# Converting the fold's 64-bit tiles in pairs of 1024 columns, with the buffers around them laid out in pairs

## The chip, the cores and the metric

One core of one Trainium2 chip runs the whole kernel. The metric is device microseconds from start to end of one execution; the kernel before was timed three times. The trace is of one further execution. The engines are named as the profile names them: PE is the matrix engine, with PEld for its weight loads, DVE the vector engine, ACT the scalar engine, POOL the GpSimd engine, SP the engine whose queue issues nearly all DMA transfers.

## The reference

Attention with pooled keys and values feeds two dense layers. For 8 batches, 8 heads, 576 tokens and 64 columns per head:

```
k_p, v_p = mean over 8 neighbouring tokens of k, v        # 72 of each per head
attn = softmax(q @ k_p.T / 8); x = attn @ v_p             # laid out as 4608 tokens x 512
x = ((x @ w1) * (x @ w2) @ w3) @ w_out                    # 512 -> 1024 -> 1024 -> 512
out = square(relu(x @ w_in)) @ w_out2                     # 512 -> 2048 -> 512
```

The weights come as 64-bit floats (`setup_inputs` multiplies float32 draws by 64-bit scalars), q, k and v as 32-bit floats.

## The kernel before, in words

Every large product is made of numbers split into a high and a low part, three matmuls for each product of tiles. Since nothing stands between `w3` and `w_out`, the kernel first multiplies these two into one matrix W: this is the **fold** (`fold`, L697). Then come nine blocks of 512 tokens (`stage_ab`, L828, and `stage_w`, L862), then the second layer.

A 64-bit weight tile of 128 x 512 numbers is 512 KB. `load64` (L142) loads it as 32-bit word pairs. `words` (L149) runs two ACT instructions over it: L152 scales the high words in place, L153 writes the scaled low words into the float32 tile `w`. `join` (L155) runs three DVE instructions: L161 (shift), L162 (sign and bits together) and L164 (integer addition into `w`). Each of the five covers 512 columns.

The fold converts 32 tiles: 16 of w3, 8 of w_out and the 8 first halves (512 columns) of w1 and w2. It walks over 64 matmul positions (`mms`, L709). At each position the steps put there by `conv` (L739) are emitted, then one float32 matmul (L819, two PE instructions in the profile), then one `tick()`, which lets attention work in. A conversion is `act` (ACT), one position later the join (DVE); for w3 two more steps, `turn` (four PE transposes, L759) and `copy` (ACT, L765); for w1 and w2 `hi` (ACT cast, L770) and `lo` (DVE subtraction, L774). A tile that a matmul needs is begun at least five positions before its first use. Tiles of w1 and w2 begin at position 14 and every 6 positions after (`W12_AT`, `W12_GAP`), and `act` of conversion n issues loads up to conversion n + 3 (`PRE` = 4, L743). The queues keep one order for each engine, which the compiler's list scheduler makes from this order of emission and from when it believes each instruction to be ready.

Buffers: raw word pairs go to `x_p` (8 buffers of 4 KB per partition) until the first x tile of the attention exists, then to `sec_p` (4 of 4 KB). The float32 `w` of w3 lies in two small tiles of `tmp_p`, that of w1 and w2 in the three `cg` tiles of `tmp_p`, w_out in `prep_p`. Split w1 and w2 go to `w0_p` (8 of 4 KB). The three buffers of `raw_p` hold the k and v tiles of batches after the first (`kv_parts`, L302) and, from the end of the fold on, the raw second halves of w1 and w2 (`second_half`, L1303). Keys of batch 1 may be loaded from position 44 on (L807). Each k tile is summed over its tokens by DVE (L330), copied by POOL (L352) and transposed by PE (`pe_kt`, L381).

Attention of batch 0 runs as side work through the fold: scores, softmax (ACT L486), transposes, and products that write x (L547, L550). After the fold, around 113 us, the first block of `stage_ab` begins, with the second halves of w1 and w2 converted tile by tile beside it.

Of the kernel before, what the change touches and what calls it, by code (L numbers as in the profile page):

```python
# [8 lines left out]
F32 = mybir.dt.float32  # L9
F32R = mybir.dt.float32r  # L10
U32 = mybir.dt.uint32
# [9 lines left out]

LEAD = 3

PRE = 4

W12_AT = 14

W12_GAP = 6

LAG = 2  # L30

# [4 lines left out]
def attn_moe_moe2_kernel(  # L36
# [58 lines left out]
    at_p = tc.alloc_tile_pool(name="att", bufs=1, side="right")  # L95


# [43 lines left out]

    def load64(src, pool):  # L142

        tag = "x" if pool is x_p else "w" if pool is prep_p else "raw"
        r = pool.tile([P, TB, 2], U32, tag=tag, name="raw")
        nc.sync.dma_start(r, src.bitcast(U32).rearrange("p (c t) -> p c t", t=2))
        return r

    def words(r, w):  # L149

        hf = r.bitcast(F32)[:, :, 1]
        nc.scalar.activation(hf, hf, ACTF.Copy, scale=2.0 ** -112)  # L152
        nc.scalar.activation(w.bitcast(U32), r[:, :, 0], ACTF.Copy, scale=2.0 ** -29)  # L153

    def join(r, w):  # L155


        u = r.rearrange("p (y c) t -> p y (c t)", y=2)[:, :, :TB // 2]
        lo, hi = (r[:, :, i].rearrange("p (y c) -> p y c", y=2) for i in range(2))
        wu = w.bitcast(U32).rearrange("p (y c) -> p y c", y=2)  # L160
# [103 lines left out]

    def xt_tile(blk, c):
        if (blk, c) not in xt:
            xt[blk, c] = x_p.tile([P, 2, TB], F32R, tag="x", name=f"x_{blk}_{c}")
        return xt[blk, c]

    tasks = []  # L270
# [153 lines left out]
    def load_q(b, hf):  # L424


        if b < EARLY:
            for i in HALF[hf]:
                s1, n = QT[i]
                if b == 0:  # L430
                    if i % 2 == 0:
                        q_nat["w"] = w0_p.tile([P, 2, H, D], F32, tag="w", name="q_nat")
                    r = q_nat["w"][:, i % 2]
# [263 lines left out]
    def fold():  # L697
# [14 lines left out]
        for pos, (m, f) in enumerate(mms):  # L712
            use.setdefault(("w3", f, m // nh), pos)
            use.setdefault(("wo", m), pos)
        begin = {}
        nxt = len(mms)
        for key, pos in sorted(use.items(), key=lambda z: -z[1]):
            begin[key] = nxt = min(pos - 5, nxt - (2 if nxt > 1 else 1))
        w12 = [("w12", n, kc) for kc in range(KD) for n in range(2)]
        for j, key in enumerate(w12):  # L720
            begin[key] = W12_AT + W12_GAP * j
        convs = sorted(begin, key=lambda key: begin[key])
        raws = {}
        n_load = [0]

        def load(upto):
            while n_load[0] < min(upto, len(convs)):
                key = convs[n_load[0]]
                n_load[0] += 1
                if key[0] == "w3":  # L730
                    _, f, h = key
                    src = w3[f * P:(f + 1) * P, h * TB:(h + 1) * TB]
                elif key[0] == "wo":
                    src = wo[key[1] * P:(key[1] + 1) * P, :]
                else:
                    src = (w1, w2)[key[1]][key[2] * P:(key[2] + 1) * P, :TB]
                raws[key] = load64(src, early_pool())

        def conv(n, key):  # L739
            st = {}  # L740

            def act():
                load(n + PRE)  # L743
                if key[0] == "w3":
                    st["w"] = tmp_p.tile([P, TB], F32, tag=("gf", "a")[key[2] % 2], name="w32")
                elif key[0] == "wo":
                    y, x = divmod(key[1], 2)
                    if y not in wo_t:
                        wo_t[y] = prep_p.tile([P, 2, TB], F32, tag="w", name="wo")
                    st["w"] = wo_t[y][:, x, :]  # L750
# [4 lines left out]
            def turn():  # L755
                st["ps"] = ps = ps_mm.tile([P, TB], F32, tag="mm", name="ps_w3")
                for c in range(nh):
                    cs = slice(c * P, (c + 1) * P)
                    nc.tensor.transpose(ps[:, cs], st["w"][:, cs], ident)  # L759

            def copy():
                _, f, h = key
                if f not in w3t:
                    w3t[f] = g_p.tile([P, nm, P], F32, tag="g", name="w3t")
                nc.scalar.copy(  # L765
                    w3t[f][:, h * nh:(h + 1) * nh, :].rearrange("p m f -> p (m f)"), st["ps"])

            def hi():
                st["t"] = w0_p.tile([P, 2, TB], F32R, tag="w", name="wt")
                nc.scalar.copy(st["t"][:, 0, :], st["w"])  # L770

            def lo():
                t = st["t"]
                nc.vector.tensor_sub(t[:, 1, :], st["w"], f32(t[:, 0, :]))  # L774
                nm_ = ("w1", "w2")[key[1]]
                wt[nm_, key[2], 0] = t
                done.add((nm_, key[2], 0))

            steps = [act, lambda: join(raws.pop(key), st["w"])]
            steps += {"w3": [turn, copy], "wo": [], "w12": [hi, lo]}[key[0]]  # L780
            for x, fn in enumerate(steps):
                put(begin[key] + x, fn)

        for n, key in enumerate(convs):
            conv(n, key)

        def merged(f):
            t = wW_p.tile([P, 2, TB], F32R, tag="w", name="Wt")
# [489 lines left out]
    def po_step(i, u):  # L1278
# [21 lines left out]
            load_wide(u + len(WIDE))  # L1300
        drop((i, u))

    def second_half(x, nm_, w, kc):  # L1303

        st_ = {}
# [7 lines left out]

        def hi():

            pool, tag = (sec_p, "raw") if x < 4 else (prep_p, "w")
            wt[nm_, kc, 1] = t = pool.tile([P, 2, TB], F32R, tag=tag, name="wt2")
            nc.scalar.copy(t[:, 0, :], st_["w"])  # L1318

        def lo():  # L1320
# [66 lines left out]
    for i in range(NB):  # L1387
# [4 lines left out]
        for u in range(U1):  # L1392
# [4 lines left out]
            stage_ab(i, u)  # L1397
            if i == last and u == TB // P - 1:
                for n in ("B11", "T1", "T2", "T3"):
                    for x in range(2):  # L1400
                        x2o[n, x] = w0_p.tile([P, 2, TB], F32R, tag="w", name="x2o")
                raw_x.append(x_p.tile([P, 2, TB], F32, tag="x", name="x2r"))
# [121 lines left out]
```

## Time and profile before

| what | value |
|---|---|
| three timed runs | 1513.43, 1515.6, 1517.6 us (median 1515.6) |
| the profiled execution, its own time | 1516.18 us |
| its span, first to last instruction | 1514.4 us |
| PE busy | 1477.3 us (98%) |
| DVE, ACT, POOL busy | 998.1, 795.9, 81.2 us |
| mean granted PE clock | 0.998 |

The span is what the trace covers; 1.8 us of the profiled execution lie around it. Busy shares are means over the span: the fold is its first 113 us, and shares there differ from the mean. [...]

### The profile page before, as it was taken

The numbers are of one execution on the slowest core, as the hardware profiler recorded it, in microseconds if no ns is written. First come the engines' busy times: TensorE is split into PE (matmuls) and PEld (weight loads), VectorE is DVE, ScalarE is ACT, GpSimd is POOL, SyncE is SP. The second block draws the span as 40 slices with busy tenths as digits, with TensorE's granted clock in tenths as the row PEclk, the third lists the DMA queues.
The fourth block names the chain that finished last, engine by engine and source line by source line (L and its number), as shares of the span: only waits on it lengthen the run. The fifth ranks groups of instructions, "written<-read, shape, count | busy, mean of one in ns | idle before, by whom it ended". The sixth has DMA issues, their size and how long they took to land.

```text
span 1514.4 us, 21299 instructions
## 1 busy us (share of the span) xinstructions
PE 1477.3 (98%) x6752; PEld 1196.1 (79%) x6752; DVE 998.1 (66%) x1798; ACT 795.9 (53%) x1953; POOL 81.2 (5%) x145
## 2 busy tenths in 40 slices
PE   6899999999999999999999999999999999999998
PEld 3457788887888887888887878888888888888887
DVE  7988776777557367374266787659675967576542
ACT  6966464545435346363246764556445644554431
POOL 1011111111010011010000000000000000000000
PEclk9999999999999999999999999999999999999999
DMA  9554666757557457465349987778777877788752
GB/s 289 200 147 137 174 187 173 204 145 220 135 159 217 143 149 208 111 191 163 102 153 338 338 276 237 208 208 234 231 208 206 234 207 206 207 273 282 211 157 90
DMA packets 292783, 301.34 MB, mean 199 GB/s; under 512 B 119360, under 2 KB 184896, under 8 KB 292672
## 3 DMA queue, kind: packets, MB, share of 16 engines
q1 hardware_dynamic: 287488, 290.54, 65.8%
q10 hardware_dynamic: 5184, 9.44, 1.7%
q8 instruction: 55, 0.90, 0.3%
q14 instruction: 56, 0.46, 0.1%
HBM read 243.27 MB, written 56.62 MB: 198 GB/s over the span
## 4 chain that ended last, share of the span: by engine, by line
PE 76%; DVE 10%; ACT 6%; DMA 5%; issue 2%; SPq 1%; ACTq 0%; DVEq 0%
PE ps_w L194 20%; PE o L1231 18%; PE acc L194 9%; PE ps_a L1129 5%; PE ps_c L1129 5%; PE ps_d L1129 5%; PE ps_h L194 3%; PE o L194 3%; PE ps_b L1129 3%; PE ps_s L469 2%; DMA raw<-in_moe_w_out_dram 2%; PE ps_av L194 1%; ACT att L486 1%; PE ps_w L819 1%; DVE raw L162 1%
## 5 line engine op out<-in xcount | busy, mean ns | idle before, releaser
L1231 PE MATMUL o<-gt,un 128*128 128x512 f32 x1344 | 330.0, 390 | 0.7 <-DVE gt L122 0.3
L1231 PEld LDWEIGHTS o<-gt,un 128*128 128x128 f32 x1344 | 251.6, 188 | 55.7 <-DVE gt L122 3.1
L122 DVE TENSOR_TENSOR gt<-gs,gt 128x512 fp32r<-128x512 f32 x240 | 164.6, 688 | 180.4 <-ACT gt L121 178.8
L194 PE MATMUL ps_w<-x,wt 128*128 128x512 f32 x960 | 235.9, 395 | 0.9 <-ACT wt L1318 0.8
L121 ACT CAST gt<-gs 128x512 fp32r<-128x512 f32 x240 | 148.5, 620 | 153.4 <-PE o L1231 86.7
L194 PE MATMUL acc<-gt,Wt 128*128 128x512 f32 x864 | 216.1, 393 | 0.0
L194 PEld LDWEIGHTS ps_w<-x,wt 128*128 128x128 f32 x960 | 176.5, 188 | 37.3 <-ACT wt L1318 1.6
L194 PE MATMUL ps_w<-x,un 128*128 128x512 f32 x768 | 184.6, 392 | 0.0
L194 PEld LDWEIGHTS acc<-gt,Wt 128*128 128x128 f32 x864 | 159.1, 188 | 30.8
L194 PEld LDWEIGHTS ps_w<-x,un 128*128 128x128 f32 x768 | 142.6, 188 | 28.9
L486 ACT ACTIVATE att<-ps_s,mx 128x72 f32<-128x72 f32 (+1 forms) x320 | 97.9, 324 | 48.9 <-DVE mx L484 48.4
L1136 ACT ACTIVATE r<-r 128x512 f32<-128x512 f32 x96 | 60.6, 632 | 106.5 <-DVE r L1166 106.2
L856 DVE TENSOR_TENSOR gf<-asb,ps_w 128x512 f32<-128x512 f32 x72 | 49.1, 682 | 90.3 <-PE ps_w L194 82.1
L1129 PE MATMUL ps_c<-x2o,un 128*128 128x512 f32 x384 | 97.9, 390 | 1.0 <-DVE u L1160 1.0
L1129 PE MATMUL ps_a<-x2o,un 128*128 128x512 f32 x384 | 97.8, 390 | 1.0 <-ACT r L1136 0.5
L1129 PE MATMUL ps_d<-x2o,un 128*128 128x512 f32 x384 | 97.5, 389 | 0.0
L1137 ACT ACTIVATE gs<-r 128x512 f32<-128x512 f32 x144 | 89.9, 629 | 1.9 <-ACT r L1136 0.3
L121 ACT CAST gt<-gf 128x512 fp32r<-128x512 f32 x72 | 44.8, 622 | 86.2 <-DVE gf L856 86.1
L1205 DVE TENSOR_TENSOR gs<-gs 128x512 f32<-128x512 f32 x128 | 86.4, 683 | 0.0
L1129 PEld LDWEIGHTS ps_c<-x2o,un 128*128 128x128 f32 x384 | 71.8, 188 | 17.0 <-DVE u L1160 2.2
L1129 PEld LDWEIGHTS ps_a<-x2o,un 128*128 128x128 f32 x384 | 71.8, 188 | 16.9 <-ACT r L1136 1.2
L1129 PEld LDWEIGHTS ps_d<-x2o,un 128*128 128x128 f32 x384 | 72.0, 188 | 15.1 <-DVE r L1166 0.2
(114 smaller groups left out, 1964.2 us busy)
## 6 DMA issues: line engine op xcount, KB each, us to landing
un<-u_w SPq DMA_DIRECT2D x128, 256.0 KB, 3.1
un<-u_A SPq DMA_DIRECT2D x128, 256.0 KB, 3.3
un<-u_S SPq DMA_DIRECT2D x128, 256.0 KB, 3.2
un<-u_oS SPq DMA_DIRECT2D x128, 256.0 KB, 3.1
un<-u_oA SPq DMA_DIRECT2D x96, 256.0 KB, 3.0
raw<-in_moe_w_dram SPq DMA_DIRECT2D x32, 512.0 KB, 5.6
raw<-in_moe_w_out_dram SPq DMA_DIRECT2D x24, 512.0 KB, 5.5
kv<-in_k_dram SPq DMA_DIRECT2D x32, 256.0 KB, 3.2
```

Source lines behind the costliest of these rows:

```text
L121: nc.scalar.copy(hi, src)
L122: return (eng or nc.vector).tensor_sub(lo, src, f32(hi))
L162: nc.vector.scalar_tensor_tensor(u, hi, 0x80000000, lo, op0=ALU.bitwise_and, op1=ALU.bitwise_or)
L194: (lambda a=a, b=b, i=i: nc.tensor.matmul(ps, a, b, start=first and i == 0, stop=last and i == n - 1))
L469: nc.tensor.matmul(ps[:n, x * 2 * SP:(x + 1) * 2 * SP], t[:, hp, c0:c0 + n], kbd[:, hp].rearrange("p a s -> p (a s)"), start=True, stop=True)
L486: nc.scalar.activation(av[:, h0 + h], sv[:, h], ACTF.Exp, bias=mx[:n, h:h + 1], scale=scale, accum_out=sm[:n, h0 + h:h0 + h + 1])
L856: front["dve"] = nc.vector.tensor_mul(gf, asb, pss[1])
L1129: nc.tensor.matmul(ps, l, r, start=first and j == 0, stop=j == len(todo) - 1, skip_group_check=True)
L1136: nc.scalar.activation(t, src, ACTF.Relu)
L1137: nc.scalar.activation(take(name), t, ACTF.Square)
L1205: d = nc.vector.tensor_sub(src, a, src)
L1231: nc.tensor.matmul(ob[x][o], l, r, start=u == 0 and m != 5 and j == 0, stop=u == NU - 1 and j == 2, skip_group_check=True)
```

## The change

Of the 32 conversions of the fold, 28 are made two at a time, by the same five instructions over 1024 columns. Four tiles stay single: the first of w3, the first two of w_out, and the last of the first three strips of w3. So 18 conversions take the place of 32, ordered by the list `heads`. A pair is loaded by two DMA transfers of 512 KB into one 8 KB buffer (`load64s`; a single tile takes an 8 KB buffer too). A w3 pair is turned and copied half by half in successive positions; a w1/w2 pair (the same rows of both) is split by one cast and one subtraction over 1024 columns. The float32 `w` of w3 pairs and of w1/w2 pairs now lies in `raw_p`. A pair begins at least five positions before the first use of its first half. `PRE` counts conversions beyond the next, `W12_AT` and `W12_GAP` are 17 and 12.

The pools `x_p`, `w0_p` and `sec_p` have half the buffers at twice the size: x tiles, q of batch 0, split weights, second halves of w1/w2, and, late in the kernel, the operands of the second layer (`x2o`) lie in pairs.

```
-PRE = 4
-W12_AT = 14
-W12_GAP = 6
+PRE = 2
+W12_AT = 17
+W12_GAP = 12
...
-    x_p = ctx.enter_context(tc.tile_pool(name="x", bufs=2 * KD))
+    x_p = ctx.enter_context(tc.tile_pool(name="x", bufs=KD))
...
-    w0_p = tc.alloc_tile_pool(name="w0", bufs=2 * KD)
+    w0_p = tc.alloc_tile_pool(name="w0", bufs=KD)
...
-    sec_p = tc.alloc_tile_pool(name="sec", bufs=4)
+    sec_p = tc.alloc_tile_pool(name="sec", bufs=2)
...
+    def load64s(srcs, pool):
+
+        r = pool.tile([P, 2 * TB, 2], U32, tag="x" if pool is x_p else "raw", name="raw")
+        for n, src in enumerate(srcs):
+            nc.sync.dma_start(
+                r[:, n * TB:(n + 1) * TB], src.bitcast(U32).rearrange("p (c t) -> p c t", t=2))
+        return r[:, :len(srcs) * TB]
...
-        nc.scalar.activation(w.bitcast(U32), r[:, :, 0], ACTF.Copy, scale=2.0 ** -29)
+        lo = r[:, :, 0]
+        if len(w.shape) == 3:
+            lo = lo.rearrange("p (y c) -> p y c", y=2)
+        nc.scalar.activation(w.bitcast(U32), lo, ACTF.Copy, scale=2.0 ** -29)
...
+        heads = [[("w3", 0, 0)], [("wo", 0)], [("w3", f, 0) for f in range(1, LEAD)], [("wo", 1)],
+                 [("w3", f, 1) for f in range(LEAD - 1)], [("w3", LEAD - 1, 1)]]
+        heads += [[("wo", m), ("wo", m + 1)] for m in range(2, nm, 2)]
+        heads += [[("w3", f, h) for h in range(2)] for f in range(LEAD, U1)]
...
+        for g in sorted(heads, key=lambda g: -min(use[x] for x in g)):
+            pos = min(use[x] for x in g)
+            nxt = min(pos - 5, nxt - (2 * len(g) if nxt > 1 else 1))
+            begin[tuple(g)] = nxt
+        for kc in range(KD):
+            begin[("w12", 0, kc), ("w12", 1, kc)] = W12_AT + W12_GAP * kc
...
-                load(n + PRE)
-                if key[0] == "w3":
-                    st["w"] = tmp_p.tile([P, TB], F32, tag=("gf", "a")[key[2] % 2], name="w32")
+                load(n + 1 + PRE)
+                if kind == "w3":
+                    if len(g) == 1:
+                        st["w"] = tmp_p.tile([P, TB], F32, tag="gf", name="w32")
+                    else:
+                        st["w"] = raw_p.tile([P, 2, TB], F32, tag="raw", name="w32")
...
-                    st["w"] = tmp_p.tile([P, TB], F32, tag="cg", name="w32", bufs=3)
-                words(raws[key], st["w"])
+                    st["w"] = raw_p.tile([P, 2, TB], F32, tag="raw", name="w32")
+                words(raws[g], st["w"])
...
+            steps = [(0, act), (1, lambda: join(raws.pop(g), st["w"]))]
+            if kind == "w3":
+                for x in range(len(g)):
+                    steps += [(2 + x, lambda x=x: turn(x)), (3 + x, lambda x=x: copy(x))]
+            elif kind == "w12":
+                steps += [(2, hi), (3, lo)]
...
-        load(5)
+        load(4)
...
+                t = x_p.tile([P, 2, 2, TB], F32, tag="x", name="x2r")
+                raw_x.append(t[:, 0])
+                more = t[:, 1]
                 for n in ("B21", "B22", "T4"):
+                    t = x_p.tile([P, 2, 2, TB], F32R, tag="x", name="x2o")
                     for x in range(2):
-                        x2o[n, x] = x_p.tile([P, 2, TB], F32R, tag="x", name="x2o")
-                more = x_p.tile([P, 2, TB], F32, tag="x", name="gx")
+                        x2o[n, x] = t[:, x]
```

## Rows read from the trace of the kernel before

**Rows 1.** The page's first part: busy time of each engine over the span.

```profile
span 1514.4 us, 21299 instructions
PE 1477.3 (98%) x6752; PEld 1196.1 (79%) x6752; DVE 998.1 (66%) x1798; ACT 795.9 (53%) x1953; POOL 81.2 (5%) x145
```

**Rows 2.** Busy time by stretch: start:end, length, each engine's us, clock, DMA.

```profile
20.00:52.00 32.00, 26.83 (x94) 14.27 (x94) 28.21 (x54) 24.50 (x71) 3.36 (x6) 0.95 0.87 294
52.00:101.00 49.00, 45.18 (x175) 24.29 (x175) 47.60 (x100) 41.47 (x117) 7.83 (x11) 1.00 0.53 168
...
113.00:165.00 52.00, 48.70 (x244) 38.37 (x243) 44.90 (x87) 33.77 (x105) 7.40 (x13) 1.00 0.54 151
165.00:1514.00 1349.00, 1337.11 (x6162) 1106.09 (x6160) 856.73 (x1519) 677.18 (x1612) 59.97 (x105) 1.00 0.68 200
...
40.00:101.00 61.00, 54.93 (x207) 28.93 (x205) 59.41 (x121) 51.70 (x142) 7.83 (x11) 1.00 0.59 192
```

**Rows 3.** The timeline of PE: start, length, instruction, idle time before it.

```profile
32.92 5.42 PE L819 MATMUL ps_w<-wo,w3t 128*128 128x512 f32 x12 [0.57 <-DVE wo L164]
...
42.44 1.12 PE L819 MATMUL ps_w<-wo,w3t 128*128 128x512 f32 x2 [0.96 <-ACT w3t L765]
...
52.03 2.84 PE L819 MATMUL ps_w<-wo,w3t 128*128 128x512 f32 x6 [1.29 <-DVE wo L164]
...
96.55 0.66 PE L390 MATMUL ps_kt<-ident,kp 128*128 128x128 f32 x4 [0.43 <-POOL kp L352]
```

**Rows 4.** The timeline of DVE: conversions, and first and last sum of k.

```profile
31.45 0.69 DVE L162 SCALAR_TENSOR_TENSOR raw<-raw 128x512 uint32<-128x512 uint32 x1
32.18 0.69 DVE L164 CUSTOM_DVE_ANT_0 wo<-raw,wo 128x1024 uint16<-128x1024 uint16 x1
...
36.60 0.69 DVE L162 SCALAR_TENSOR_TENSOR raw<-raw 128x512 uint32<-128x512 uint32 x1
37.20 0.42 DVE L161 TENSOR_SCALAR raw<-raw 128x512 uint32<-128x512 uint32 x1
37.54 0.69 DVE L164 CUSTOM_DVE_ANT_0 w<-raw,w 128x1024 uint16<-128x1024 uint16 x1
...
86.20 1.03 DVE L330 TENSOR_REDUCE kp<-kv 128x64 f32<-128x512 f32 x1
...
97.01 1.03 DVE L330 TENSOR_REDUCE kp<-kv 64x64 f32<-64x512 f32 x1
```

**Rows 5.** Busy time by stretch of line L161 alone (one in each join), DVE.

```profile
40.00:101.00 61.00, 8.22 (x20) 1.00 0.59 192
```

**Rows 6.** Groups by line and shape, 20 to 113 us: busy, mean ns, idle before.

```profile
L122 DVE TENSOR_TENSOR aT<-ps_t,aT 128x512 fp32r<-128x512 f32 x3 | 2.0, 666 | 0.1
L550 DVE TENSOR_TENSOR x<-ps_av,x 128x256 fp32r<-128x256 f32 x8 | 3.4, 420 | 0.5 <-ACT x L547 0.4
L547 ACT CAST x<-ps_av 128x256 fp32r<-128x256 f32 x8 | 2.9, 365 | 1.0 <-PE ps_av L534 1.0
...
L122 DVE TENSOR_TENSOR aT<-ps_t,aT 128x384 fp32r<-128x384 f32 x2 | 1.1, 552 | 0.0
...
L547 ACT CAST x<-ps_av 128x64 fp32r<-128x64 f32 x4 | 0.9, 220 | 0.0
L550 DVE TENSOR_TENSOR x<-ps_av,x 128x64 fp32r<-128x64 f32 x4 | 0.9, 214 | 0.0
```

**Rows 7.** The timeline of ACT: two conversion instructions in a row.

```profile
40.09 0.69 ACT L152 ACTIVATE raw<-raw 128x512 f32<-128x512 f32 x1
40.67 0.68 ACT L153 ACTIVATE wo<-raw 128x512 uint32<-128x512 uint32 x1
```

**Rows 8.** The timeline of SP's queue: DMA issues, start, length, tile, count.

```profile
54.64 1.52 SPq L320 DMA_DIRECT2D kv<-in_k_dram  x3
...
90.54 0.48 SPq L320 DMA_DIRECT2D kv<-in_k_dram  x1
```

**Rows 9.** DMA issues, 0 to 125 us: count, KB each, us to landing.

```profile
kv<-in_k_dram SPq DMA_DIRECT2D x8, 256.0 KB, 4.4
```

More of the change, by code (lines that the diff above doesn't have):

```diff
@@ L142, in load64 @@
     def load64(src, pool):
-        tag = "x" if pool is x_p else "w" if pool is prep_p else "raw"
+        tag = "w" if pool is prep_p else "raw"
         r = pool.tile([P, TB, 2], U32, tag=tag, name="raw")
@@ L266, in xt_tile @@
         if (blk, c) not in xt:
-            xt[blk, c] = x_p.tile([P, 2, TB], F32R, tag="x", name=f"x_{blk}_{c}")
+            t = x_p.tile([P, 2, 2, TB], F32R, tag="x", name=f"x_{blk}_{c // 2}")
+            for x in range(2):
+                xt[blk, c // 2 * 2 + x] = t[:, x]
         return xt[blk, c]
@@ L430, in load_q @@
                 if b == 0:
-                    if i % 2 == 0:
-                        q_nat["w"] = w0_p.tile([P, 2, H, D], F32, tag="w", name="q_nat")
-                    r = q_nat["w"][:, i % 2]
+                    if i % 4 == 0:
+                        q_nat["w"] = w0_p.tile([P, 4, H, D], F32, tag="w", name="q_nat")
+                    r = q_nat["w"][:, i % 4]
                 else:
@@ L714, in fold @@
             use.setdefault(("wo", m), pos)
+        heads = [[("w3", 0, 0)], [("wo", 0)], [("w3", f, 0) for f in range(1, LEAD)], [("wo", 1)],
+                 [("w3", f, 1) for f in range(LEAD - 1)], [("w3", LEAD - 1, 1)]]
+        heads += [[("wo", m), ("wo", m + 1)] for m in range(2, nm, 2)]
+        heads += [[("w3", f, h) for h in range(2)] for f in range(LEAD, U1)]
+        assert sorted(k for g in heads for k in g) == sorted(use)
         begin = {}
         nxt = len(mms)
[L717 to L722, printed above, removed]
+        for g in sorted(heads, key=lambda g: -min(use[x] for x in g)):
[4 more added lines that the diff above has]
+            begin[("w12", 0, kc), ("w12", 1, kc)] = W12_AT + W12_GAP * kc
+        convs = sorted(begin, key=lambda g: begin[g])
         raws = {}
@@ L727, in load @@
             while n_load[0] < min(upto, len(convs)):
-                key = convs[n_load[0]]
+                g = convs[n_load[0]]
                 n_load[0] += 1
-                if key[0] == "w3":
[L731 to L736, printed above, removed]
@@ L737, in load @@
-                raws[key] = load64(src, early_pool())
-        def conv(n, key):
+                srcs = []
+                for key in g:
+                    if key[0] == "w3":
+                        _, f, h = key
+                        srcs.append(w3[f * P:(f + 1) * P, h * TB:(h + 1) * TB])
+                    elif key[0] == "wo":
+                        srcs.append(wo[key[1] * P:(key[1] + 1) * P, :])
+                    else:
+                        srcs.append((w1, w2)[key[1]][key[2] * P:(key[2] + 1) * P, :TB])
@@ L748, in act @@
                     if y not in wo_t:
                         wo_t[y] = prep_p.tile([P, 2, TB], F32, tag="w", name="wo")
-                    st["w"] = wo_t[y][:, x, :]
+                    st["w"] = wo_t[y][:, x, :] if len(g) == 1 else wo_t[y]
                 else:
-                    st["w"] = tmp_p.tile([P, TB], F32, tag="cg", name="w32", bufs=3)
-                words(raws[key], st["w"])
-            def turn():
-                st["ps"] = ps = ps_mm.tile([P, TB], F32, tag="mm", name="ps_w3")
+                    st["w"] = raw_p.tile([P, 2, TB], F32, tag="raw", name="w32")
@@ L757, in turn @@
+                words(raws[g], st["w"])
+            def turn(x):
+                w = st["w"] if len(g) == 1 else st["w"][:, x, :]
+                st["ps", x] = ps = ps_mm.tile([P, TB], F32, tag="mm", name="ps_w3")
                 for c in range(nh):
                     cs = slice(c * P, (c + 1) * P)
-                    nc.tensor.transpose(ps[:, cs], st["w"][:, cs], ident)
-            def copy():
-                _, f, h = key
+                    nc.tensor.transpose(ps[:, cs], w[:, cs], ident)
@@ L763, in copy @@
+            def copy(x):
+                _, f, h = g[x]
                 if f not in w3t:
@@ L765, in copy @@
                 nc.scalar.copy(
-                    w3t[f][:, h * nh:(h + 1) * nh, :].rearrange("p m f -> p (m f)"), st["ps"])
+                    w3t[f][:, h * nh:(h + 1) * nh, :].rearrange("p m f -> p (m f)"), st["ps", x])
             def hi():
-                st["t"] = w0_p.tile([P, 2, TB], F32R, tag="w", name="wt")
-                nc.scalar.copy(st["t"][:, 0, :], st["w"])
+                st["t"] = w0_p.tile([P, 2, 2, TB], F32R, tag="w", name="wt")
+                nc.scalar.copy(st["t"][:, :, 0, :], st["w"])
             def lo():
                 t = st["t"]
[L774 to L785, printed above, removed]
+                nc.vector.tensor_sub(t[:, :, 1, :], st["w"], f32(t[:, :, 0, :]))
+                for _, x, kc in g:
+                    nm_ = ("w1", "w2")[x]
+                    wt[nm_, kc, 0] = t[:, x]
+                    done.add((nm_, kc, 0))
+            steps = [(0, act), (1, lambda: join(raws.pop(g), st["w"]))]
[4 more added lines that the diff above has]
+                steps += [(2, hi), (3, lo)]
+            for x, fn in steps:
+                put(begin[g] + x, fn)
+        for n, g in enumerate(convs):
+            conv(n, g)
         def merged(f):
@@ L1301, in po_step @@
         drop((i, u))
+    wide2 = {}
     def second_half(x, nm_, w, kc):
@@ L1314, in hi @@
         def hi():
-            pool, tag = (sec_p, "raw") if x < 4 else (prep_p, "w")
-            wt[nm_, kc, 1] = t = pool.tile([P, 2, TB], F32R, tag=tag, name="wt2")
+            if x < 4:
+                if x % 2 == 0:
+                    wide2[kc] = sec_p.tile([P, 2, 2, TB], F32R, tag="raw", name="wt2")
+                t = wide2[kc][:, x % 2]
+            else:
+                t = prep_p.tile([P, 2, TB], F32R, tag="w", name="wt2")
+            wt[nm_, kc, 1] = t
             nc.scalar.copy(t[:, 0, :], st_["w"])
```

19 lines of the change are left out of this document (12 added, 7 removed).

## The prediction

> **What bounds the kernel now.** I read the page's first part first. PE is busy for 1477.3 of 1514.4 us [rows 1], so all of its idle time is 37.1 us, and nothing that leaves PE's work alone can give more than that. The change leaves PE's work alone: the same 64 transposes and 64 fold matmuls are issued. So the question is where PE idles. The table by stretch answers it [rows 2]: from 165 us on PE idles 11.9 us in 1349, from 113 to 165 us 3.3, from 52 to 101 us 3.8, from 20 to 52 us 5.2. The reader is to see beside this that from 40 to 101 us DVE is busy for 59.41 of 61 us, while PE is busy for 54.93 and ACT for 51.70. DVE is the engine without slack in the larger part of the fold, and PE, at 90%, stands close behind it. A DVE saving there is worth its own size at first, and never more than PE's 6.1 us of idle time in that stretch. PE's timeline shows what such idle time looks like: 1.29 us before a matmul at 52.03 that waited for DVE's join of w_out, 0.96 at 42.44 for ACT's copy of turned w3, 0.57 at 32.92 for a join [rows 3].
>
> **DVE, per instruction.** A pair takes three DVE instructions in place of six, and the subtraction of a w1/w2 pair one in place of two. That is 14 x 3 + 4 = 46 instructions fewer, for the same number of columns. What one instruction costs beyond its columns the trace does not show at 1024 columns of these operations, so I bound it. Two instructions that don't depend on each other start 0.60 us apart (36.60 to 37.20) although the first is said to last 0.69 [rows 4]. From 64 to 256 columns a subtraction grows from 214 to 420 ns, 1.07 ns a column; from 384 to 512 another grows from 552 to 666, 0.89 a column [rows 6]. Taken from 0.60 us, 512 columns at these rates leave 0.05 or 0.14 us of fixed cost. I take 0.07, near the lower end, because the row behind that end has the wider span of columns. The sum is 46 x 0.07 = 3.2 us, bounds 2.3 and 6.4. Of the 32 joins 20 start between 40 and 101 us [rows 5], so 10 pairs, 30 instructions, fall where DVE is the bound: 2.1 us.
>
> **DVE, waits inside a join.** An instruction that needs the one ahead of it starts later: L162 to L164 is 0.73 us (31.45 to 32.18) against 0.60 [rows 4]. There are two such links in a join and half as many joins. All 20 links saved in the bound stretch at 0.13 would give 2.6 us. But mostly another instruction stands between, as L161 between L162 and L164 at 37.20, so the low bound is zero and I take a third: 0.8 us.
>
> The trace so shows an overlap of 0.09 us between independent instructions. [...]
>
> **ACT.** A pair takes two instructions in place of four, and a w1/w2 pair one cast in place of two: 32 fewer. L152 and L153 start 0.58 us apart [rows 7]. A cast grows from 220 to 365 ns between 64 and 256 columns, 0.76 a column [rows 6], which leaves 0.19 us fixed; the lower bound is zero. The sum lies between 0 and 6.1 us. I take 0.1 each, 3.2 us, and count none of it toward the end: ACT has 9 us of slack from 40 to 101 us [rows 2] and DVE's work lies over it. Without DVE's cover it would be worth its size.
>
> **Longer steps.** This is the loss in the change. The first half of a pair waits for both: ACT works about 1.0 us longer and DVE 1.5 before the first can be used (the second tile's own instructions, at the starts in [rows 4, 7]). The first pair that PE stands before is w_out's third and fourth tile, for which it waited until 32.92 [rows 3]. With the pair the matmul starts about 2.2 us later (0.9 on ACT, 1.3 on DVE, after the savings above). Then the fourth tile is there too, and the waits of 0.96 and 1.29 us that came next are swallowed: by 52 us the delay is back at zero. I cost it at nothing, with 2.2 us as the upper bound. The later pairs repeat the pattern; DVE does a tile ahead of need once, then the second half is free. If the waits behind it weren't there, 2.2 us would stay.
>
> **Moved loads.** The 32 loads of the fold remain, 512 KB each, on SP's queue, in nearly the same order. A single tile fills a buffer of 8 KB, so that somewhat less is loaded ahead. I cost it at nothing: by 54.64 us SP had run so far ahead that it was issuing k tiles of batch 1, 32 us before DVE first summed one at 86.20 [rows 4, 8]. Past SP's queue nothing else moves; POOL's has only k copies and attention.
>
> **raw_p.** The eleven pairs of w3 and w1/w2 take turns in the three buffers that k tiles of batch 1 use. Before, three k loads went out at 54.64 into fresh buffers; the last went at 90.54 and its sum ran at 97.01 [rows 4, 8]. After, k tiles come when pairs let go and land in 4.4 us [rows 9]. Two at a time they keep pace: each sum 2.7 us behind the last (half of 4.4 to land and 1.0 to sum), the first at 86.20 as before, the last ends at 86.20 + 1.03 + 4 x 2.7 = 98.0. The sums then end when they did. Cost nothing, upper bound in the rival below. What waits behind them: PE's k transposes, which already waited 0.43 us for POOL at 96.55 [rows 3].
>
> **Laying out in pairs.** x, q of batch 0, split weights and x2o have as many bytes as before, are written by the same instructions and freed by the same steps, at most one product later. Those late in the kernel lie beside PE at 99% [rows 2]. Nothing, with 1 us either way as the scheduler orders anew.
>
> **Sum.** 2.1 + 0.8 = 2.9 us off the 1516.18 of the profiled execution, 1513.3. That execution lies 0.6 above the median of the three, so for the median 1515.6 - 2.9 = 1512.7 us. From 101 us on PE sets the pace and only starts earlier.
>
> **Rivals.** *The forecast*: 2.9 us faster, chance 0.38. A measurement of this kernel can tell about 0.3%, 4.5 us, from no change, so this counts as the same.
>
> *Fixed cost high, PE's waits go with it*, chance 0.27. With 0.14 us an instruction 30 x 0.14 = 4.2 us go, and with links and a share of the 5.2 us between 20 and 52 us two thirds of PE's idle time up to 101 us, 6 of 9.0: 1509.6. For it: every wait in rows 3 ahead of 96 us is for a join or its ACT work. Against it: PE's idle time there is 9.0 us in all, and between 52 and 101 us it is only 3.8, in many small pieces.
>
> *Amortized already*, chance 0.20: 1024 columns cost twice 512, or the longer steps give back what is saved. The change then doesn't do what it is for: 1515.6.
>
> *k comes late*, chance 0.13, the other side. The mechanism sits in raw_p: pairs hold two buffers, and k's five tiles go one after another through the third. Each takes 4.4 us to land and 1.0 to sum [rows 4, 9]. If the first keeps its place, the others follow 5.4 us apart and the last ends at 86.20 + 1.03 + 4 x 5.4 = 108.8 us, where it ended at 98.0. PE's transposes of k come 10.8 us late. With the 2.9 saved that is 1523.5. It decides from where k's sums end 2.9 + 4.5 us late, after about 105.4. Against it: with two buffers nothing is late, as worked out above, and PE has fold matmuls that the scheduler can put ahead.
>
> **Numbers.** The remaining 0.02 is for a reordered later stage. Faster by over 0.3%: 0.27 and the forecast's own upper end, 0.30. Slower: 0.13 and the 0.02, 0.15. Within: 0.55. The range reaches from 9 us of vanished PE idle time (1506.6, say 1507) to most of the late k, 1521; its worst end is left out.
>
> **What would show it.** Right: DVE's conversion lines at 1024 columns, 1.13 us apart for L162 and 0.60 for L161; DVE busy some 3 us less up to the first `stage_ab` matmul, and that matmul at about 110 us rather than 113. If pairs cost 1.20 or more, the saving was not there. If PE's k transposes start after 100 us with DVE's sums waiting for DMA, it is the last rival. If the first pair's wait is longer than 2.2 us and later ones don't shrink, the steps were too long. If the fold ends earlier and the total does not, the stage from 113 to 165 us, with DVE busy 44.90 of 52 [rows 2], took it back.

## The result, and the profile after

The changed kernel is slower. Its median is 1526.87 us over six runs (1524.59 to 1528.5), against 1515.32 us over six runs of the kernel before: 11.6 us more, ratio 1.008 [1.007, 1.009]. The prediction was 1512.7 us with a range to 1521, so the time lies outside the range, on the side that had a chance of 0.15. The profiled execution of the changed kernel took 1528.5 us itself, with a span of 1526.7 us, 12.3 us more than the span before.

The page's first part, after:

```profile
span 1526.7 us, 21229 instructions
PE 1484.2 (97%) x6752; PEld 1200.5 (79%) x6752; DVE 990.6 (65%) x1752; ACT 793.5 (52%) x1921; POOL 79.3 (5%) x145
```

Against [rows 1], DVE has its 46 instructions less and ACT its 32, and both are busy for less time. PE has the same 6752 matmuls and is busy for 6.9 us longer. Its idle time also grows, from 37.1 to 42.5 us. In two of the stretches below the granted clock is lower as well, 0.93 where it was 0.98 and 0.98 where it was 1.00.

To see where the 12.3 us lie I cut both spans at the same four events: the first matmul of `stage_ab`, the first `ps_a` matmul of the second layer, its first matmul into `o`, and the end. Each stretch then holds the same PE work. Busy time by stretch (start:end, length, each engine's us, clock, DMA share, GB/s) of the kernel before:

```profile
0.00:112.73 112.73, 91.25 (x349) 51.37 (x349) 96.20 (x195) 84.99 (x236) 13.71 (x28) 0.98 0.68 214
112.73:801.50 688.77, 680.45 (x3311) 565.03 (x3310) 430.11 (x867) 333.23 (x1065) 67.53 (x117) 1.00 0.59 166
801.50:886.70 85.20, 83.18 (x361) 66.97 (x361) 61.19 (x106) 60.75 (x113) 0.00 (x0) 1.00 1.00 346
886.70:1514.40 627.70, 622.44 (x2737) 512.73 (x2736) 410.59 (x632) 316.97 (x542) 0.00 (x0) 1.00 0.74 213
```

The same view of the kernel after:

```profile
0.00:116.60 116.60, 94.78 (x348) 55.31 (x349) 90.78 (x149) 82.67 (x204) 12.09 (x28) 0.93 0.65 206
116.60:803.00 686.40, 679.77 (x3312) 564.94 (x3310) 421.12 (x854) 328.02 (x1057) 67.22 (x117) 1.00 0.58 162
803.00:898.00 95.00, 87.05 (x362) 67.56 (x361) 69.74 (x123) 66.14 (x120) 0.00 (x0) 0.98 0.98 335
898.00:1526.70 628.70, 622.63 (x2737) 512.72 (x2735) 408.99 (x629) 316.71 (x541) 0.00 (x0) 1.00 0.74 214
```

The reader is to see two losses. The fold is 3.87 us longer (112.73 to 116.60), 2.37 of which come back in the long stretch behind it. The third stretch, the head of the second layer, is 9.80 us longer (85.20 to 95.00). It lies 690 us behind the code that was to become faster. The last stretch adds 1.0.

**The head.** Before it begins, DVE and the DMA engines do less than they did. The stretch from 750 to 800 us, before and then after:

```profile
750.00:800.00 50.00, 50.00 (x223) 41.38 (x222) 27.82 (x46) 20.26 (x35) 0.00 (x0) 1.00 0.51 164
```

```profile
750.00:800.00 50.00, 50.00 (x222) 41.42 (x221) 17.87 (x29) 14.80 (x26) 0.00 (x0) 1.00 0.34 100
```

What is missing is conversions of the second layer's output weights. A few of their raw tiles had been loaded earlier, before 670 us in both kernels. The next left SP's queue at 772.24 us before, and at 800.50 after, 28 us later (SP's timeline):

```profile
772.24 0.37 SPq L146 DMA_DIRECT2D raw<-in_moe_w_out_dram  x1
```

```profile
800.50 0.33 SPq L146 DMA_DIRECT2D raw<-in_moe_w_out_dram  x1
```

So the conversions fall into the third stretch, where DVE is busy for 69.7 us instead of 61.2 and ACT for 66.1 instead of 60.8. The DMA engines have no time left there to make the late start good: their share was 1.00 before already and is 0.98 after. PE waits more. Its waits from 690 to 900 us, after:

```profile
PE ps_c L1162 <- DMA un<-u_S: 2.2, 2, 1.9
PE ps_b L1162 <- DVE raw L174: 2.1, 1, 2.1
PE ps_a L1162 <- DMA un<-u_A: 1.5, 2, 1.0
```

Before, no PE wait in this stretch was for a DMA, and the longest line of the view was 1.0 us. In the third stretch PE's idle time grows by 5.9 us (2.02 to 7.95). The other 3.9 us of the 9.8 are longer busy time with the same matmuls: the mean granted clock fell to 0.98, and behind a wait of 2.1 us the slice from 828 to 832 us was granted 0.67. How much of the 3.9 us is the clock, these views don't show.

**The fold.** Its idle time is the same, 112.73 - 91.25 = 21.5 us before and 116.60 - 94.78 = 21.8 after. What PE waited for has changed. From the view of PE's waits up to the first `stage_ab` matmul, before and then after:

```profile
PE ps_w L819 <- ACT w3t L765: 3.7, 6, 1.0
PE ps_w L819 <- DVE wo L164: 1.9, 2, 1.3
PE ps_w L759 <- DVE w L164: 1.3, 2, 0.8
...
PE ps_w L759 <- ACT w L153: 0.7, 1, 0.7
```

```profile
PE ps_t L531 <- ACT att L501: 3.1, 1, 3.1
PE ps_s L484 <- ACT att L501: 2.5, 1, 2.5
...
PE ps_w L787 <- DVE w L177: 1.3, 2, 1.0
...
PE ps_w L787 <- ACT w3t L793: 0.2, 1, 0.2
...
PE ps_w L852 <- ACT w3t L793: 0.2, 1, 0.2
```

The waits for conversions fell from 7.6 us to 1.7. In their place stand two long waits put down to softmax, and the clock. The granted clock by slices of 4 us, after:

```profile
24.00:28.00 4.00, 3.75 (x11) 2.50 (x12) 4.00 (x11) 2.33 (x11) 1.61 (x3) 0.50 1.03 389
...
36.00:40.00 4.00, 4.00 (x11) 2.12 (x10) 3.93 (x5) 3.73 (x6) 0.00 (x0) 0.66 0.63 183
...
56.00:60.00 4.00, 0.88 (x5) 0.70 (x4) 3.76 (x5) 3.95 (x15) 0.00 (x0) 0.91 0.96 355
60.00:64.00 4.00, 3.35 (x14) 2.56 (x14) 2.89 (x6) 3.73 (x11) 1.46 (x3) 0.50 0.96 274
64.00:68.00 4.00, 4.00 (x8) 1.56 (x7) 2.62 (x4) 4.00 (x6) 0.16 (x1) 0.74 0.81 235
```

PE was idle for 2.48 us before 21.40 and for 3.12 us before 59.33. From 24 to 28 and from 60 to 64 us it was granted 0.50. Before, the slice from 20 to 24 us was granted 0.57 and every later one of the fold 1.00. Over the whole fold the mean granted clock fell from 0.98 to 0.93, and PE was busy for 3.5 us more with the same matmuls.

### The profile page after: what moved, and what is told of

The parts are those of the page before. It is cut to its first block, busy times and chain, and to the rows that moved or that the text cites. A ratio compares the mean times of both kernels' runs of the same rounds, so it can differ in the third digit from the quotient of the medians.

```text
span 1526.7 us, 21229 instructions
## 1 busy us (share of the span) xinstructions
PE 1484.2 (97%) x6752; PEld 1200.5 (79%) x6752; DVE 990.6 (65%) x1752; ACT 793.5 (52%) x1921; POOL 79.3 (5%) x145
## 4 chain that ended last, share of the span: by engine, by line
PE 82%; DVE 8%; DMA 4%; ACT 3%; issue 2%; SPq 1%; POOL 0%; ACTq 0%; DVEq 0%; POOLq 0%
PE ps_w L207 22%; PE o L1264 18%; PE acc L207 11%; PE ps_c L1162 5%; PE ps_a L1162 5%; PE ps_d L1162 4%; PE ps_h L207 3%; PE ps_w L852 3%; PE o L207 3%; PE ps_b L1162 2%; PE ps_s L484 2%; PE ps_av L207 2%; PE ps_t L531 1%; DVE raw L175 1%; DVE gt L122 1%
## 5 line engine op out<-in xcount | busy, mean ns | idle before, releaser
L885 ACT COPY asb<-ps_w 128x512 f32<-128x512 f32 x72 | 42.5, 590 | 84.3 <-PE ps_w L207 81.9
```

Source lines behind the costliest of these rows:

```text
L885: nc.scalar.copy(asb, ps)
```

## The experiments

Ten kernels ran. In what follows the position p of the fold means its matmul number p, counted from 0 in the order of `mms`; the first `stage_ab` matmul is the fold's end. Fold ends and stretches come from one execution of each kernel. Kernels with the same fold show how far to trust them: it ends at 112.7 us before, 113.1 in e2 and 112.8 in e6, and at 116.6 after and 116.0 in e1.

**1. The x2o tiles regrouped (e1).** When the second layer's operands `x2o` are cut, the x tiles of block 7 are free, those of block 8 not yet: four buffers of 4 KB. Before, the scheduler gave them to raw x, both halves of B21 and the first half of B22. After, they are two pairs, and go to (x2r, gx) and to B21; B22 has to wait for block 8. DVE's timeline agrees: the last splits into `x2o` come behind a pause, and they are three before (two from 802.44 us, one at 804.25) and four after (two each from 799.77 and 801.58). Cutting the first half of B22 (with a subtraction for T4) is what frees a buffer of `raw_p`, and the output weights load into `raw_p`. This kernel pairs the tiles otherwise, so that the first half of B22 lies in the second free pair:

```diff
-                for n in ("B21", "B22", "T4"):
-                    t = x_p.tile([P, 2, 2, TB], F32R, tag="x", name="x2o")
-                    for x in range(2):
-                        x2o[n, x] = t[:, x]
+                for x in range(2):
+                    t = x_p.tile([P, 2, 2, TB], F32R, tag="x", name="x2o")
+                    x2o["B21", x] = t[:, 0]
+                    x2o["B22", x] = t[:, 1]
+                t = x_p.tile([P, 2, 2, TB], F32R, tag="x", name="x2o")
+                for x in range(2):
+                    x2o["T4", x] = t[:, x]
```

> The changed kernel, with the late operand tiles grouped otherwise: the first halves of B21 and B22 share one 8 KB tile, the second halves the next, so that B22's first half lies in a buffer that block 7 leaves free, as before the change. Buffer theory (B22's first half waits for block 8's x, that keeps a raw_p buffer, and w_out's conversions start 28 us late): first matmul of the second layer's output step at about 888 us instead of 898.0, total 1516 to 1518 us. Fold theory (the loss is made in the fold, and what is lost around 850 us only follows from its shifted order): total stays at 1525 to 1527.

Measured: 1518.37 us, ratio 1.003 [1.0017, 1.0043] to before, 8.5 us less than after. SP's timeline and the third stretch of this kernel:

```profile
776.51 0.37 SPq L146 DMA_DIRECT2D raw<-in_moe_w_out_dram  x1
```

```profile
803.10:888.60 85.50, 83.23 (x361) 66.96 (x360) 58.97 (x103) 60.17 (x111) 0.00 (x0) 1.00 0.99 341
```

The load is back within 5 us of its old place and the head takes 85.5 us. The rest of the changed layout stayed, so the loss in the head hangs on this one grouping.

**2. The same wait put into the kernel before (e6).** The fold is untouched; only the two halves of B22 are cut in the other order, so that the first half is again the late one:

```diff
-            for i in range(2):
+            for i in ((1, 0) if name == "B22" and p == 0 else (0, 1)):
```

> The kernel before, with the two halves of B22 cut in the other order for the first pair of blocks: its second half takes the last buffer that block 7 leaves free, and its first half waits for block 8. Nothing else is touched, the fold least of all. (The line moved in the run before this one turned out to change no buffer: they are given out at first use.) Buffer theory: raw_p is not freed, w_out's loads start near 800 us instead of 772, first matmul of the output step at 895 to 898 us instead of 886.7, total 1523 to 1526. Fold theory: 1514 to 1517.

Measured: 1526.26 us, ratio 1.0076 [1.0061, 1.0091]: 11.1 us slower than before, as slow as the change. SP's timeline and the third stretch:

```profile
797.12 1.01 SPq L146 DMA_DIRECT2D raw<-in_moe_w_out_dram  x2
```

```profile
800.30:893.70 93.40, 84.85 (x361) 66.48 (x360) 69.14 (x123) 66.19 (x120) 0.00 (x0) 1.00 0.98 334
```

One cut in the wrong order costs nearly as much as the whole change. With e1 this shows the cause of the head's loss from both sides. The sizes are rougher: the traced execution of e6 was the fastest of its four, 8.0 us above the traced one before, and 8.2 of these are in the head.

What holds PE in the head is not the DMA engines alone. PE's waits from 690 to 900 us in e6:

```profile
PE ps_b L1129 <- DVE raw L161: 2.2, 1, 2.2
...
PE ps_a L1129 <- DMA un<-u_A: 1.1, 2, 0.7
```

Its waits for DMA come to 1.8 us in this view, those for DVE to 6.9, and the longest ends with the shift of a conversion (L161), as the one of 2.1 us after does (L174). So the late conversions seem to hold PE through DVE as well as through the DMA engines, and no run separates the two.

**3. A first try at that, which tested nothing (e2).** The line that allocates gx was moved ahead of the others, to take the free buffer from B22:

```diff
                 raw_x.append(x_p.tile([P, 2, TB], F32, tag="x", name="x2r"))
+                more = x_p.tile([P, 2, TB], F32, tag="x", name="gx")
                 for n in ("B21", "B22", "T4"):
...
-                more = x_p.tile([P, 2, TB], F32, tag="x", name="gx")
```

> The kernel before, with one line moved: the tile gx is allocated ahead of B21, so that both halves of B22 get buffers that block 8 still uses. Fold and layout of 4 KB are as before. Buffer theory: w_out's conversions start only after the last block, the stretch from 800 to 900 us loses some 9 us, total 1523 to 1526. Fold theory: no difference, 1514 to 1517.

Measured: 1514.14 us, ratio 0.9999 [0.999, 1.0009], with this load at 772.06 us. The order of the lines did not move the buffers. e6, which turns the order of use, did, so they seem to go to whichever tile is used first. So e2 says nothing on either theory, and e6 took its place.

**4. The width alone (e3).** e1 with every pair converted as two halves of 512 columns; loads, buffers and positions as in e1, and the cast and subtraction of w1 and w2 still at 1024:

```diff
-                words(raws[g], st["w"])
+                for x in range(len(g)):
+                    words(*half(x))
...
+            def joins():
+                for x in range(len(g)):
+                    join(*half(x))
...
-            steps = [(0, act), (1, lambda: join(raws.pop(g), st["w"]))]
+            steps = [(0, act), (1, joins)]
```

> e1 with each pair's words and join done as two sets of 512 columns, in the same buffers, from the same loads, at the same positions; cast and subtraction of w1/w2 stay at 1024. Long-step theory of the fold: the first half of a pair is ready earlier, the first stage_ab matmul comes at about 113 us rather than 116.6, total 2 to 3 us below e1. Saving theory: DVE has 2.7 us more work, first stage_ab matmul at 118 to 120, total 1 to 3 us above e1.

Measured: 1520.50 us, ratio 1.0044 [1.0029, 1.0059]; the fold ends at 119.3 us, against 116.0 in e1. So 1024 columns are worth 3.3 us at the end of the fold; in the total it is 2.1 us, with intervals that overlap. The first stretch, of e3 and then of e1:

```profile
0.00:119.30 119.30, 91.42 (x349) 51.66 (x349) 95.77 (x191) 85.33 (x232) 16.42 (x28) 0.96 0.64 202
```

```profile
0.00:116.00 116.00, 94.06 (x349) 53.80 (x349) 90.92 (x149) 82.44 (x204) 12.09 (x28) 0.93 0.65 208
```

The wide form takes 5.9 us from PE's idle time (27.9 to 21.9) and gives 2.6 back as busy time at a lower clock.

**5. raw_p (e5).** e3, with the float32 `w` back in its old tiles of `tmp_p`, so that `raw_p` holds k and v alone:

```diff
-                    if len(g) == 1:
-                        st["w"] = tmp_p.tile([P, TB], F32, tag="gf", name="w32")
-                    else:
-                        st["w"] = raw_p.tile([P, 2, TB], F32, tag="raw", name="w32")
+                    st["w"] = [tmp_p.tile([P, TB], F32, tag=("gf", "a")[key[2] % 2], name="w32")
+                               for key in g]
...
-                    st["w"] = raw_p.tile([P, 2, TB], F32, tag="raw", name="w32")
+                    st["w"] = [tmp_p.tile([P, TB], F32, tag="cg", name="w32", bufs=3) for _ in g]
```

> e3 with the 32-bit tiles of w3 and w1/w2 back in the small tiles of the kernel before, so that raw_p is left to k and v; cast and subtraction of w1/w2 at 512 columns too. What is left of the change in the fold is the paired loads into 8 KB buffers and the new positions. raw_p theory: k tiles of batch 1 are issued at about 55 us again, PE's transposes of k come 3 to 4 us earlier than in e3, total 2 to 4 us below e3. If raw_p is covered: within 1 us of e3.

Measured: 1518.04 us, ratio 1.0026 [1.0013, 1.0039]; fold end 115.6, 3.7 us before e3's (the intervals of the totals overlap). Its first three k loads go out at 56.91 us, against 54.64 before the change. So in the narrow form `raw_p` seems to cost the fold 3.7 us. The hi and lo instructions also differ here (two of 512 for one of 1024), so this is not the buffer alone.

**6. Tiles of w1 and w2 later (e7).** The matmul at position 24 is the first of w3's strip 3 (the fourth). Before, the joins from position 13 up to that matmul's were those of w_out's seventh and eighth tile, one tile of w1 and the strip's first half. After, it is both tiles of w_out, a whole pair (w1, w2) begun at 17, and both halves of the strip: two tiles more. e7 is e1 with that pair moved behind the strip:

```diff
-W12_AT = 17
+W12_AT = 24
-W12_GAP = 12
+W12_GAP = 10
```

> e1 with the w1/w2 pairs begun at positions 24, 34, 44 and 54 instead of 17, 29, 41 and 53. Front-loading theory (ahead of position 24 DVE has to finish w_out's last pair, a whole w1/w2 pair and both halves of w3's fourth strip, two tiles more than before, and this makes the step of 5 us that e1, e3 and e5 all lose between positions 24 and 27): position 27 comes at 61 to 64 us instead of 66.3, first stage_ab matmul at 112 to 114, total 1515 to 1517. Rival, long steps spread over the fold: position 27 stays within 1 us, total 1517.5 to 1519.

Measured: 1517.58 us, ratio 1.0012 [1.0004, 1.0021]; fold end 112.8, as before the change. These are start times in us of the fold's matmul by position, worked out from PE's timelines (two instructions make one matmul, and a group of n is divided evenly):

```
position  before  after    e1    e3    e7   e10   e11
       3    25.3   28.4  27.5  25.3  27.8  24.4  25.2
       6    32.9   36.5  36.1  33.3  35.6  36.6  33.2
      12    39.7   45.7  45.5  42.5  44.4  47.1  48.7
      21    52.0   53.6  53.4  51.5  52.6  55.0  58.0
      24    56.9   63.6  63.3  60.9  56.9  59.3  61.5
      33    69.0   75.2  75.2  73.8  70.5  71.1  72.7
      48    90.9   96.7  97.1  97.0  91.5  92.4  92.9
      63   110.8  114.7 114.1 117.4 110.9 111.0 112.5
```

The jump from 21 to 24 is 10.0 us after the change, 4.9 before and 4.3 in e7. The timeline of DVE after shows what filled it:

```profile
47.50 1.22 DVE L177 CUSTOM_DVE_ANT_0 wo<-raw,wo 128x2048 uint16<-128x2048 uint16 x1
48.63 0.70 DVE L174 TENSOR_SCALAR raw<-raw 128x1024 uint32<-128x1024 uint32 x1
49.23 0.49 DVE L379 SCALAR_TENSOR_TENSOR vl<-vp,rows,vl 128x256 fp32r<-128x256 f32 x1
49.63 1.23 DVE L175 SCALAR_TENSOR_TENSOR raw<-raw 128x1024 uint32<-128x1024 uint32 x1
50.77 1.89 DVE L341 TENSOR_REDUCE v<-kv 32x128 f32<-32x1024 f32 x1
52.59 1.20 DVE L177 CUSTOM_DVE_ANT_0 w<-raw,w 128x2048 uint16<-128x2048 uint16 x1
53.72 0.47 DVE L379 SCALAR_TENSOR_TENSOR vl<-vp,rows,vl 128x256 fp32r<-128x256 f32 x1
...
55.92 1.23 DVE L802 TENSOR_TENSOR wt<-w,wt 128x1024 fp32r<-128x1024 f32 x1 [0.37 <-ACT wt L798]
57.07 0.69 DVE L174 TENSOR_SCALAR raw<-raw 128x1024 uint32<-128x1024 uint32 x1
...
60.34 1.21 DVE L177 CUSTOM_DVE_ANT_0 w<-raw,w 128x2048 uint16<-128x2048 uint16 x1
```

The join whose last step starts at 52.59 and the subtraction at 55.92 are the pair of w1 and w2. The strip's join begins behind them at 57.07 and its last step ends at 61.55. ACT meanwhile waited for a sum of v, which DVE began at 50.77 (49.47 before). ACT's and PE's timelines, after:

```profile
52.69 0.40 ACT L378 ACTIVATE vr<-v,rows 32x128 fp32r<-32x128 f32 x1 [3.61 <-DVE v L341]
```

```profile
45.74 10.47 PE L852 MATMUL ps_w<-wo,w3t 128*128 128x512 f32 x24
59.33 1.09 PE L531 MATMUL ps_t<-ident,att 128*128 128x128 f32 x4 [3.12 <-ACT att L501]
...
61.70 1.94 PE L787 MATMUL ps_w<-ident,w 128*128 128x128 f32 x8
...
63.65 5.66 PE L852 MATMUL ps_w<-wo,w3t 128*128 128x512 f32 x10
```

The view puts PE's idle time of 3.12 us down to softmax, since the softmax transposes stand next in its queue. But the turn at 61.70 could not have come before the strip's join in any case: the join is what holds the fold. In e7 the strip's join has its last step at 52.87 on DVE, PE turns the strip at 54.24, and the softmax transposes come at 59.44, no earlier than here, with fold matmuls ahead of them. There the slice from 60 to 64 us is granted in full:

```profile
60.00:64.00 4.00, 3.35 (x13) 1.51 (x12) 3.69 (x4) 4.00 (x7) 2.46 (x3) 1.00 1.01 396
```

Of the 3.2 us won in the fold only 0.8 show in the medians, whose intervals overlap: in e7 the head takes 87.4 us (800.8 to 888.2, granted clock 0.98) where e1's took 85.5 at 1.00. Why, these runs don't show.

**7. raw_p again, in the wide form (e9).** e7 with the float32 `w` in the old tiles; the scaling, shift and sign step stay at 1024 columns, the others go back to 512 (the addition shown, of the others the like):

```diff
+                    for x in range(2):
+                        wu = st["w"][x].bitcast(U32)
+                        nc.vector.tensor_add(wu, wu, u[:, x])
```

> e7 with the 32-bit tiles of w3 and w1/w2 in the small tiles of the kernel before; of a pair's instructions the scaling of high words, the shift and the joining of sign and bits stay 1024 wide, the low words and the addition are two of 512, cast and subtraction too. raw_p theory: k of batch 1 is issued near 55 us, its transposes come 2 to 4 us earlier than in e7, total 1 to 3 us below e7. Saving theory: DVE has 1.3 us more work, total 0.5 to 1.5 above e7.

Measured: 1517.03 us, ratio 1.0013 [1.0004, 1.0022], fold end 113.6. That is 0.5 us under e7 with overlapping intervals, and mixes a free `raw_p` with more instructions. It decides nothing, except that `raw_p` holds no large loss here.

**8. Single tiles where PE stands waiting (e8, e10, e11).** Three trials to give the first half of a pair back its head start. e8 is e7 with the two halves of strip 3 single:

```diff
-        heads += [[("w3", f, h) for h in range(2)] for f in range(LEAD, U1)]
+        heads += [[("w3", f, h) for h in range(2)] for f in range(LEAD + 1, U1)]
+        heads += [[("w3", LEAD, h)] for h in range(2)]
```

> e7 with the fourth strip of w3 converted as two single tiles, begun at positions 19 and 23 as before the change. Front-loading theory: another 1.5 to 2.5 us less at position 27, which then comes at 59 to 61 us as before the change, total 1 to 2 us below e7. Rival: no change against e7, within 1 us.

e10 is e7 with the first w3 pair single, loaded as far ahead as in the kernel before:

```diff
-        heads = [[("w3", 0, 0)], [("wo", 0)], [("w3", f, 0) for f in range(1, LEAD)], [("wo", 1)],
+        heads = [[("w3", 0, 0)], [("wo", 0)], [("w3", 1, 0)], [("w3", 2, 0)], [("wo", 1)],
...
-        load(4)
+        load(5)
```

> e7 with the very first pair (the second and third strip of w3) made single again, as before the change. In e7 ACT runs 2.1 us for this pair ahead of the softmax that PE's scores wait for (2.92 us idle at 21.13), and position 6 comes at 35.6 us against 32.9 before. First-pair theory: position 3 at 25 to 26 us instead of 27.8, position 6 at 33 to 34, first stage_ab matmul 1 to 2.5 us earlier than in e7, total 1514.5 to 1516.5. Rival, DVE catches it up by position 24 anyway: position 24 and the total as in e7 within 0.7 us.

e11 is e10 with w_out's third and fourth tile single as well:

```diff
-        heads += [[("wo", m), ("wo", m + 1)] for m in range(2, nm, 2)]
+        heads += [[("wo", 2)], [("wo", 3)]]
+        heads += [[("wo", m), ("wo", m + 1)] for m in range(4, nm, 2)]
```

> e10 with w_out's third and fourth tile single too. First-pair theory: position 6 at 32.5 to 33.5 us as before the change; if DVE's saving in the other pairs then shows, the first stage_ab matmul comes at 110 to 112 us and the total at 1513 to 1515, below the kernel before. Rival: the same end as e7, 1516.5 to 1518.

Measured: e8 1515.89 us, 1.0004 [0.9994, 1.0014], fold end 113.4; e10 1516.11 us, 1.0013 [1.0004, 1.0022], fold end 112.9; e11 1515.74 us, 1.0007 [0.9998, 1.0015], fold end 114.4. In the table e10 gains 3.4 us on e7 at position 3 and e11 2.4 at position 6, and both have lost it, and more, by position 12. A single tile takes a whole 8 KB buffer, so later loads would come later; that is an argument, not a test. e8's median lies 1.7 us under e7's, but the intervals overlap and its fold is no shorter (113.4 against 112.8). No kernel of this study is faster than the one before; e8 and e11 cannot be told from it.

## Why the prediction was wrong

**Laying out in pairs: the step that failed.** It costed the new layout at nothing, 1 us either way, because x and x2o have as many bytes, are written by the same instructions, and "Those late in the kernel lie beside PE at 99%". It measured 8.5 us when taken back (e1) and 11.1 when put into the old kernel (e6). Two things were not asked. The first is what a pair does to lifetimes: a buffer of two tiles is free only when both are, and four free tiles that the scheduler hands out one by one became two that it hands out as they were paired. The second is who waits behind: B22's cut holds a buffer of `raw_p`, and with it the loads of the output weights. The row to look at was there. The 99% of [rows 2] is a mean over 1349 us; cut at the head of the second layer it shows a DMA share of 1.00 for 85 us, a stretch with no DMA time in reserve. With this fell the last sentence of the sum too, that from 101 us on PE sets the pace: PE's idle time in these 85 us went from 2.02 to 7.95 us, in a stretch that is now 95.

**Longer steps: the second step that failed.** They were costed at nothing, with 2.2 us as the upper bound, and the fold ends 3.9 us later. The first pairs do make PE start later, by more and sooner than the sum had it: 3.1 us at position 3 already, behind the pair of w3's second and third strip. In e10, where that pair is single, and in e3, where its halves are converted one by one, position 3 is at or before its old place. At position 6 the delay is 3.6 us, and at position 12 it is 6.0. Only then does it shrink, to 1.6 us at position 21, as forecast. "The later pairs repeat the pattern" was wrong too. Which tiles DVE must finish ahead of a given position was never counted. By the order of emission it is two more for position 12 (w_out's sixth, and the second strip's second half), and two more for position 24, where the delay jumps to 6.7 us. e7 takes the second two away and ends the fold at 112.8.

**The DVE and ACT terms were right for one instruction.** From [rows 4], 512 columns of the shift cost 0.34 us between starts (37.20 to 37.54, where the profile lets it last 0.42) and the sign step 0.60. After, 1024 columns cost 0.60 (48.63 to 49.23) and 1.14 (49.63 to 50.77), and the addition 1.13. So an instruction saved is worth 2 x 0.34 - 0.60 = 0.08 for the shift and 2 x 0.60 - 1.14 = 0.06 for the sign step; 0.07 was taken. DVE's busy time up to the first `stage_ab` matmul fell by 5.4 us (96.20 to 90.78), where some 3 was given as a sign. On ACT:

```profile
29.11 1.17 ACT L160 ACTIVATE raw<-raw 128x1024 f32<-128x1024 f32 x1
30.13 1.18 ACT L164 ACTIVATE wo<-raw 128x1024 uint32<-128x1024 uint32 x1
```

1.02 us against 2 x 0.58 in [rows 7] is 0.14 saved, where 0.1 was taken. And a saving did reach PE: e3 against e1 shows 3.3 us at the end of the fold for both engines together, where the sum had 2.9 for DVE. The waits put down to conversions shrank by 5.9 us, but of these 3.1 came back under softmax's name, in a wait that e7 shows to be a join's as well. The sum failed in what it set against the saving.

**raw_p: no cost seen in this form, and the rival's mechanism did not occur.** *k comes late* had 1523.5 us, the number nearest to the measured one; that it came so near is luck. The k loads do go out later, and PE's transposes of k do not wait for them (SP's and PE's timelines, after):

```profile
82.28 0.34 SPq L335 DMA_DIRECT2D kv<-in_k_dram  x1
...
92.20 1.47 SPq L335 DMA_DIRECT2D kv<-in_k_dram  x2
```

```profile
100.68 0.60 PE L405 MATMUL ps_kt<-ident,kp 128*128 128x128 f32 x4
```

In [rows 3] the same transposes came at 96.55 with a wait of 0.43. Now they are 4.1 us later and have none: PE was itself 4 to 6 us behind by then. The sign that the prediction gave for this rival was met in its words all the same, since the transposes start after 100 us and one of DVE's sums of k, at 98.45, waited 0.97 us for its DMA. But the sums end at 101.5 us, well short of the 105.4 from which it was to decide. In the narrow form (e5) a freed `raw_p` seems to gain 3.7 us, so the pool may not be free of cost in every form.

**What stayed open.** e1 still loses 3.3 us in the total (1518.37 against 1515.06) and e7 2.4, although e7's fold is as short as before. The 3.3 us and e6's 11.1 make 14.4, where the change cost 11.6, so the sizes of the parts hold to some 3 us only. The old assignment of the four free buffers itself was not tried with pairs: it would put operands and plain float32 x data into one buffer.

## What to carry to other kernels

When two tiles are merged into one buffer, list every buffer of that pool in the whole kernel, who is given it when it comes free, and which load waits behind that: the price stood 690 us away from the edit, and one late cut of one tile cost 8 to 11 us. When work is done in larger pieces by position, count for each consumer how many pieces now stand before it on the engine, and not the mean load. And look for the stretch that has little in reserve (here one with DMA at a share of 1.00) rather than at a mean over the long stage around it.

## What the runs showed of the hardware that was not expected

The fold lost more than PE's waits account for. In the fold after, PE idled as long as before (21.8 and 21.5 us) but in longer pieces (3.12 and 2.48 us where none before was above 1.63, the first wait of each span left aside), and its matmuls took 3.5 us more. The 3.12 us before 59.33 stand ahead of a slice at 0.50, and the ten matmul instructions from 63.65 took 0.57 us each where the 24 from 45.74 took 0.44. In e7 that wait is gone, the slice from 60 to 64 us was granted 1.00, and the fold's busy time is 90.95 us with 21.9 us of idle time.

So the same sum of idle time went with different clocks, which the prediction, with its one sum, did not ask about. When the clock falls is not settled by these traces. Before, the slice from 20 to 24 us was granted 0.57 although none of PE's waits from 12 to 24 us was longer than 0.90. And two waits of 1.18 and 0.92 us stand ahead of the slice from 36 to 40 us both after, where it was granted 0.66 and the six matmul instructions from 36.51 took 0.66 us each, and in e7, where the twelve from 35.57 took 0.45.
